# Score masks through two 64x128 array tiles in place of four 64x64 ones, and a new order of the same steps, in an attention and adapter kernel

## The chip, the core and the metric

The kernel runs on one core of a Trainium2 chip. The metric is the device time of one execution in microseconds. Three runs of the kernel before took 101.26, 102.77 and 100.77 us; the median is 101.26 us.

Five engines of the core work side by side, each through its own list of instructions: PE (matrix multiplication; its weight loads are shown as a row of their own, PEld), DVE (vector work), ACT (activation functions and copies), POOL (general work; here also the queue that issues the input loads) and SP (here only a DMA queue). They wait for one another by semaphores. PE writes into eight banks of accumulators (PSUM), 128 partitions by 512 fp32 values each.

## The reference

Eight batches, eight heads, 576 positions, head size 64. Attention looks back over a short window: heads 0 to 3 over the 32 positions up to the own one, heads 4 to 7 over every fourth of the last 128. The result goes through a mixture of eight low-rank adapters, of which each row takes its two best.

```python
rel = pos[:, None] - pos[None, :]
mask_plain = (rel >= 0) & (rel < window)                               # window 32
mask_dil = (rel >= 0) & (rel < window * dilation) & (rel % dilation == 0)  # dilation 4
scores = np.where(masks[None, :, :, :], scale * q @ k.T, -1e9)
attn = softmax(scores);  x = attn @ v          # then (B, S, H*D) -> rows of 512
logits = x @ w_gate;     w = softmax over the two largest logits
out = x + sum over the two chosen e of w[e] * ((x @ A[e]) @ B[e])      # rank 16
```

(`softmax` and the last line are shortened from longer code.)

## The kernel before

The host sorts the positions of the dilated heads by their remainder by four. A dilated window then looks like a plain one of 32 neighbours, cut at the borders of the four classes. So both kinds of head are a band: 64 keys against the 96 queries that can see them, nine such blocks per head, and a block's mask is a 64x96 pattern of 0 and -30000. `plain` holds the pattern twice, on partitions 0 to 63 and 64 to 127; `MD` holds nine copies for the dilated heads with the cuts put in. `CON` also holds a 128x128 identity, used to put masks into the banks and to transpose.

Work is cut by batch r (0 to 7) and head group g (0 plain, 1 dilated; four heads each). The two halves of the partitions hold two heads' keys and queries each. The steps have names, which the order and the prediction use:

- `gRGH`, `qRGH`, `vRGH`: loads of batch R, group G, half H, fp32 in memory and bf16 on chip, issued by POOL. At most eight are in flight. Three slots hold batches; batch r waits for the readers of batch r-3.
- `S0 r.g`, `S1 r.g`: scores of blocks 0 to 4 and 5 to 8, into a pair of banks, on PE. First come the masks (identity times pattern, starting the accumulation), then the score matmuls of 64x64 tiles, four tiles side by side (two heads by two partition halves).
- `E0`, `E1`: exponentials on ACT, from the pair of banks to the probabilities P (four buffers).
- `Va`, `Vb`: probabilities times values on PE, 128x128 tiles, the row sums in an extra column; `H`: the last 64 rows of a batch, in 128x64 tiles.
- `R`, `N` (`RH`, `NH`): reciprocal of the row sums and normalisation on DVE; `B`, `BH`: cast to bf16 on POOL.
- `T`, `TH` transposes on PE, `C`, `CH` their copies on ACT; `Z` the router and the adapters' A on PE, `ZC` its copies on ACT; `M`, `s12`, `tt`, `top`, `g2` the choice of the two best on DVE, `th` on ACT; `gz` the gated product on POOL; `GT`, `gc`, `gn` its transpose and copies; `D` the adapters' B on PE, `A` the addition on DVE.
- `st`: five stores on SP (batches 0 to 3, 4 and 5, 6, and 7 in two pieces), issued behind the last loads.
- Start-up: `con`, `bt` (SP) and `aw` (ACT) load constants and weights, `md` builds `MD` on DVE, `zero..`, `pz..`, `gz0.`, `xz.`, `fz` clear what must be zero.

The order of all steps is written out in the table `ORDER` (lines 52 to 89); `name@bank` says which bank a step takes. `replay` (line 154) walks the table and gives each engine its instructions in this order, so an engine never overtakes. While it does so it estimates times, only to decide where to put fillers: matmuls on zeros (`fz`) that stand in PE's list where PE is expected to be idle (`fill`, line 279). The cost terms in the code (`t`, `wired`) act on nothing else once the table is given.

All instructions are emitted through a helper, so the profile puts all of them on line 120; the tiles' names tell them apart (`con` or `md,con` into `ps`: masks; `kv` into `ps`: scores; `kv,p`: values; `aw,xt`: router and A; `bt,gn` and `bt,gc`: B; `fz`: filler).

Of the kernel before, what the change touches and what calls it, by code (L numbers as in the profile page):

```python
# [11 lines left out]
BF = mybir.dt.bfloat16  # L12
# [5 lines left out]
B, H, S, D = 8, 8, 576, 64  # L18
# [5 lines left out]
SEG = 96  # L24
PER = 192
CI = S // C
VW = D + 1
# [22 lines left out]
GZSPLIT = ()  # L50

ORDER = """
startACT aw land_aw startDVE zero01 zero11 pz00 pz30 pz11 pz20 gz00 pz21 zero00 startSP con land_con fz awc bt
land_bt xz0 md startPOOL g011 land_g011 g010 land_g010 S0_0.1@0 S1_0.1@2 pz10 q001 land_q001 E0_0.1 Va_0.2@0
q000 land_q000 v001 land_v001 E1_0.1 pz01 Vb_0.2 R_0.2 N_0.2 v000 land_v000 S0_0.0@2 g101 land_g101 S1_0.0@4
Va_0.3@6 g100 land_g100 Vb_0.3 E0_0.0 Va_0.0@2 g110 land_g110 g111 land_g111 E1_0.0 g200 land_g200 Va_0.1@0
g201 land_g201 Vb_0.0 zero10 R_0.0 g211 land_g211 table N_0.0 g210 land_g210 Vb_0.1 H_0@4 B_0.2 RH_0 NH_0 BH_0
TH_0@4 CH_0 btc R_0.1 N_0.1 S0_1.0@2 E0_1.0 S1_1.0@4 B_0.0 E1_1.0 R_0.3 N_0.3 B_0.1 T0_0@6 B_0.3 g301
land_g301 T1_0@7 C1_0 pz31 Va_1.1@2 g300 land_g300 Va_1.0@0 zero20 Vb_1.1 xz1 C0_0 Vb_1.0 S0_1.1@4 E0_1.1
R_1.1 N_1.1 Z0_0@6 ZC0_0 Z1_0@2 g311 land_g311 R_1.0 N_1.0 ZC1_0 B_1.1 M0_0 M1_0 top_0 s12_0 S1_1.1@4 E1_1.1  # L60
B_1.0 T0_1@6 g310 land_g310 tt_0 th_0 Va_1.2@2 g2_0 zero21 Va_1.3@0 Vb_1.2 R_1.2 gz0_0 N_1.2 Vb_1.3 R_1.3
N_1.3 S0_2.0@4 H_1@7 RH_1 B_1.2 NH_1 C0_1 S1_2.0@2 GT_0@6 B_1.3 gc_0 E0_2.0 E1_2.0 Va_2.0@4 Va_2.1@0 BH_1 g401
land_g401 Vb_2.0 gn_0 R_2.0 N_2.0 g400 land_g400 TH_1@2 CH_1 T1_1@3 C1_1 Vb_2.1 R_2.1 N_2.1 B_2.0 D0p_0@6
A0p_0 S0_2.1@4 E0_2.1 Z1_1@3 S1_2.1@0 E1_2.1 B_2.1 T0_2@2 C0_2 Va_2.3@6 Va_2.2@4 Vb_2.3 g410 land_g410 R_2.3
N_2.3 Vb_2.2 R_2.2 N_2.2 Z0_1@0 ZC1_1 M1_1 H_2@1 RH_2 ZC0_1 M0_1 g411 land_g411 NH_2 S0_3.0@6 B_2.3 s12_1 tt_1
D4_0@0 A4_0 g501 land_g501 S1_3.0@4 D2p_0@2 A2p_0 B_2.2 T1_2@1 E0_3.0 E1_3.0 Va_3.0@6 gz01 Va_3.1@4 BH_2 g500
land_g500 C1_2 th_1 Vb_3.0 top_1 g2_1 TH_2@0 CH_2 Vb_3.1 S0_3.1@2 R_3.1 R_3.0 N_3.0 N_3.1 E0_3.1 Z0_2@0 ZC0_2
M0_2 S1_3.1@6 E1_3.1 Z1_2@2 g511 land_g511 ZC1_2 gz0_1 GT_1@0 gc_1 gn_1 M1_2 s12_2 top_2 tt_2 th_2 Va_3.3@4
Va_3.2@6 Vb_3.3 R_3.3 Vb_3.2 B_3.1 B_3.0 T0_3@2 C0_3 R_3.2 N_3.3 S0_4.0@0 E0_4.0 N_3.2 g510 land_g510 H_3@3
RH_3 D2p_1@4 D4_1@2 S1_4.0@6 E1_4.0 g2_2 B_3.3 NH_3 g601 land_g601 A2p_1 A4_1 D0p_1@0 A0p_1 B_3.2 T1_3@3 C1_3  # L70
Va_4.1@4 Va_4.0@6 g600 land_g600 BH_3 TH_3@2 CH_3 Vb_4.1 Vb_4.0 R_4.1 R_4.0 N_4.0 S0_4.1@0 E0_4.1 gz0_2 GT_2@2
gc_2 gn_2 Z0_3@3 ZC0_3 N_4.1 M0_3 Z1_3@6 ZC1_3 M1_3 s12_3 Va_4.3@0 S1_4.1@4 g611 land_g611 E1_4.1 top_3 tt_3
th_3 D0p_2@2 A0p_2 S0_5.0@6 E0_5.0 B_4.1 B_4.0 g610 land_g610 g2_3 Va_4.2@4 Vb_4.3 gz0_3 Vb_4.2 R_4.3 N_4.3
S1_5.0@2 R_4.2 N_4.2 H_4@6 g700 land_g700 RH_4 NH_4 T0_4@7 E1_5.0 C0_4 Va_5.1@0 GT_3@2 gc_3 D4_2@3 A4_2 Vb_5.1
R_5.1 N_5.1 S0_5.1@4 D2p_2@6 B_4.3 g701 land_g701 B_4.2 T1_4@3 gn_3 D0p_3@0 E0_5.1 A2p_2 BH_4 TH_4@2 Va_5.0@4
g711 land_g711 C1_4 A0p_3 D2p_3@6 A2p_3 Vb_5.0 R_5.0 N_5.0 B_5.0 g710 land_g710 CH_4 Z1_4@2 ZC1_4 Z0_4@0 M1_4
ZC0_4 M0_4 s12_4 tt_4 S1_5.1@2 B_5.1 S0_6.0@6 Va_5.2@0 S1_6.0@4 top_4 E1_5.1 Vb_5.2 R_5.2 E0_6.0 th_4 g2_4
N_5.2 Va_5.3@2 Va_6.0@6 Vb_5.3 R_5.3 N_5.3 E1_6.0 Vb_6.0 R_6.0 N_6.0 H_5@4 RH_5 S0_6.1@0 S1_6.1@2 E0_6.1 gz0_4
GT_4@5 gc_4 E1_6.1 gn_4 Va_6.1@6 B_5.3 NH_5 B_5.2 Va_6.2@0 Vb_6.1 R_6.1 N_6.1 T0_5@2 C0_5 Vb_6.2 R_6.2 B_6.0
N_6.2 T1_5@5 C1_5 BH_5 TH_5@4 B_6.1 CH_5 D2p_4@6 B_6.2 S0_7.0@2 E0_7.0 A2p_4 Va_6.3@0 D4_3@5 Vb_6.3 A4_3 R_6.3  # L80
N_6.3 D0p_4@6 A0p_4 Z0_5@5 ZC0_5 Z1_5@2 ZC1_5 S1_7.0@0 E1_7.0 S0_7.1@4 Va_7.1@6 Va_7.0@2 Vb_7.1 B_6.3 T1_6@0
M0_5 M1_5 s12_5 tt_5 th_5 top_5 g2_5 gz0_5 Vb_7.0 R_7.1 N_7.1 B_7.1 R_7.0 N_7.0 B_7.0 E0_7.1 C1_6 S1_7.1@4
H_6@6 RH_6 GT_5@7 E1_7.1 Va_7.3@0 Va_7.2@2 Vb_7.3 T0_6@4 Vb_7.2 gc_5 gn_5 NH_6 BH_6 T0_7@5 TH_6@7 H_7@6 C0_6
R_7.3 N_7.3 B_7.3 CH_6 D0p_5@0 C0_7 R_7.2 N_7.2 Z0_6@7 RH_7 Z1_6@2 B_7.2 T1_7@3 D4_4@5 NH_7 A0p_5 ZC0_6 ZC1_6
D4_5@4 D2p_5@0 M0_6 BH_7 TH_7@2 M1_6 s12_6 tt_6 C1_7 th_6 top_6 CH_7 Z1_7@2 ZC1_7 A4_5 g2_6 gz0_6 Z0_7@4 A2p_5
ZC0_7 A4_4 GT_6@2 gc_6 gn_6 D4_6@2 M1_7 M0_7 s12_7 tt_7 th_7 top_7 g2_7 A4_6 D2p_6@4 A2p_6 st_0 land_st_0
D0p_6@0 A0p_6 st_4 land_st_4 gz0_7 GT_7@2 gc_7 gn_7 D0p_7@2 A0p_7 D2p_7@0 st_6 land_st_6 st_7a land_st_7a
A2p_7 D4_7@4 A4_7 st_7b land_st_7b
"""


def constants():
    k = np.arange(64)[:, None]
    w = np.arange(SEG)[None, :]
    m = np.where((w >= k) & (w - k < W), 0.0, NEG).astype(np.float32)
    m = np.concatenate([m, m], 0)
    return np.concatenate([m, np.eye(128, dtype=np.float32)], 1).astype(ml_dtypes.bfloat16)


class Op:  # L100
# [222 lines left out]
def attn_adapters_kernel(  # L323
# [12 lines left out]
    te, ve, se, ge, sy = (Noted(e, made) for e in (nc.tensor, nc.vector, nc.scalar, nc.gpsimd, nc.sync))  # L336
# [4 lines left out]
    def sb(shape, dt, name):  # L341
        return one.tile(shape, dt, name=name)
# [17 lines left out]
    TH = [sb([128, 5, 8], FP, f"th{i}") for i in range(2)]  # L360
    TOP = [sb([128, 5, 8], FP, f"top{i}") for i in range(2)]
    G2 = [sb([128, 5, 8], FP, f"g2{i}") for i in range(2)]
    CON = sb([128, SEG + 128], BF, "con")
    MD = sb([128, NB, SEG], BF, "md")
    FZ = sb([128, 512], BF, "fz")
    AWF = sb([128, 4 * (ER + E)], FP, "awf")
# [1 line left out]
    AW = sb([128, 4, ER + E], BF, "aw")  # L368
    BT = sb([128, H * D], BF, "bt")
    plain = CON[:, 0:SEG]  # L370
    ident = CON[:, SEG:]
    PS = [psum.tile([128, 2, 512], FP, name=f"ps{i}") for i in range(4)]

    def zero(view):
# [11 lines left out]
    add = plan.add  # L386

    def pe(cols, **kw):
        t = sum(max(c / 2400.0, 0.042) + 0.003 for c in cols)
        return dict(eng="PE", occ=t, lat=t + 0.25, **kw)  # L390
# [9 lines left out]

    wire = {"all": []}

    def wired(nbytes, pieces, issue, name, late=0.85):
        took = 0.97 * (nbytes / 438400.0 + 0.031 * pieces / 16 + 0.03)
        land = add("DMA", took, took + late, None, deps=[issue], prio=len(wire["all"]), name="land " + name)
        wire["all"].append(land)
        return land

    def early(eng, queue, dst, src, nbytes, name, deps=()):
        def emit():  # L410
            i = queue.dma_start(out=dst, in_=src)
            for d in deps:
# [7 lines left out]

    plan.first = {e: add(e, t, t, None, prio=-3000, name="start" + e)
                  for e, t in (("SP", 0.75), ("ACT", 0.72), ("POOL", 1.24), ("DVE", 0.9))}
    c_con = early("SP", sy, CON, con, 57000, "con")
    c_bt = early("SP", sy, BTF, bt, 262000, "bt")
    c_aw = early("ACT", se, AWF, aw, 278000, "aw")
    plan.first["ACT"] = add("ACT", 1.35, 1.35, None, prio=-1500, name="table")
    fz = add("DVE", 0.33, 0.45, lambda: ve.memset(zero(FZ), 0), prio=-70, name="fz")
# [54 lines left out]
    queued = []  # L482
# [3 lines left out]
    def load(r, half, c0, c1, deps, name):  # L486
        n = len(INST)
        INST[n] = None
        shift = 0 if half == 0 else QG + VN
        dst = T[r % SLOTS][(lo, hi)[half], c0:c1]  # L490
        src = rows[r, half, :, c0 - shift : c1 - shift]

        def emit():
            INST[n] = ge.dma_start(out=dst, in_=src)

        before = [queued[n - 8]] if n >= 8 else []
        issue = add("POOL", 0.55, 2.1, emit, deps=deps, prio=-1000 + n, name=name)
        issue.order_deps, issue.queued = before, True
        queued.append(wired(64 * (c1 - c0) * 4, 64, issue, name))
        return queued[-1]  # L500

    def vcols(half, g):
# [28 lines left out]
    pdone = {}  # L531
# [13 lines left out]
    def attention(r):  # L545
        for g in range(2):
# [8 lines left out]
            for part, (b0, nb) in enumerate(((0, 5), (5, 4))):  # L555
                k = Bank(2, 1)

                def scores(r=r, g=g, b0=b0, nb=nb, k=k):
                    o = pair(k)
                    for half in range(2):  # L560
                        hs = (lo, hi)[half]
                        for hh in range(2):
                            dst = o[(lo, hi)[hh], half, 0 : nb * SEG]
                            if g == 0:
                                m = plain[hs].unsqueeze(1).to_broadcast([64, nb, SEG])
                            else:
                                m = MD[hs, b0 : b0 + nb].rearrange("p b w -> p (b w)")
                            te.matmul(
                                dst, lhsT=ident[hs, 64 * half : 64 * half + 64], rhs=m,
                                start=True, stop=False, skip_group_check=True,  # L570
                            )
                    for j in range(nb):
                        b = b0 + j
                        n = SEG if b < NB - 1 else 64
# [5 lines left out]
                                    start=False, stop=(j == nb - 1), skip_group_check=True,  # L580
                                )

                t = nb * SEG / 2400 + 0.03 + nb * 0.056
                sc = add(
                    "PE", t, t + 0.25, scores, deps=klist + [c_con] + ([md] if g else []) + ([last] if last else []),
                    bank=k, prio=base + part, name=f"S{part} {r}.{g}", mode=1,
# [75 lines left out]
                        )  # L662

        base = 100.0 * r + 60
        hv = add(**pe([2 * VW] * 4), emit=halves, deps=pdone[2 * r] + pdone[2 * r + 1], bank=k, prio=base + 8, name=f"H {r}", mode=2)
        for g in range(2):
            pdone[2 * r + g].append(hv)
        att_done[r].append(hv)
# [297 lines left out]
```

## Time and profile before

| | |
|---|---|
| median of three runs | 101.26 us (100.77 to 102.77) |
| the profiled execution | 102.37 us, of which the span of the instructions is 100.6 us |
| PE busy | 83.6 us, 1577 matmuls |
| PE weight loads | 65.0 us, 1577 |
| DVE, ACT, POOL busy | 72.4, 63.5, 51.8 us |
| DMA | 24.50 MB, mean 244 GB/s |
| masks: `con` 64*64 64x480 and 64x384, `md,con` the same | 4 x 32 matmuls |
| scores: `kv` 64*64 | 576 matmuls |
| fillers: `fz` | 33 matmuls |

The profile is of one execution. It divides the span into 40 slices of 2.5 us and shows each engine's busy share in tenths. Matmuls overlap in the array and their ends are modelled, so their durations add up to more than the time they take; the distance from one start to the next says what a matmul costs. The chain of waits goes backwards from the last instruction to what released it; its shares say where time can be won or lost. A tile shape such as 64*64 means 64 rows by 64 columns of the array.

### The profile page before, as it was taken

Reading aid. Unit: us, or ns where it says so; the run is one execution under the profiler, and the core shown is the slowest. Engines: PE = TensorE matmul, PEld = TensorE weight load, DVE = VectorE, ACT = ScalarE, POOL = GpSimd, SP = SyncE. Lnnn points to the kernel's source line nnn. Section 1 sums busy time; section 2 is a strip of 40 time slices with the busy share of each in tenths; the row PEclk is TensorE's granted clock in tenths of the full one; section 3 lists DMA queues with packets and bytes.
Section 4 is the critical chain, followed back from the end, with each engine's and each line's share of the span. In section 5 each row is a group of like instructions: output and inputs, shape, how many; then the busy total and the mean of one; then the engine's idle time right before and its main releaser. Section 6 shows DMA issues by size and latency. Waiting matters only on the chain.

```text
span 100.6 us, 3747 instructions
## 1 busy us (share of the span) xinstructions
PE 83.6 (83%) x1577; PEld 65.0 (65%) x1577; DVE 72.4 (72%) x210; ACT 63.5 (63%) x109; POOL 51.8 (51%) x88
## 2 busy tenths in 40 slices
PE   0059799999999999998999999599799999887500
PEld 0021468487978978886987888387699897743300
DVE  5884012946596499877979999788698899787640
ACT  5600429299978969777797895629759998432000
POOL 5912254498797666747925940667423851531000
PEclk9999999999999999999999999999999999999965
DMA  2999999999999999999999999999459969299894
GB/s 51 311 196 189 218 215 213 208 216 219 216 213 211 210 219 213 218 211 213 211 219 219 210 210 219 210 216 214 84 238 454 425 285 469 80 410 469 352 415 171
DMA packets 3888, 24.50 MB, mean 244 GB/s; under 512 B 800, under 2 KB 800, under 8 KB 3488
## 3 DMA queue, kind: packets, MB, share of 16 engines
q0 software_dynamic: 2720, 14.23, 69.3%
q1 hardware_dynamic: 1008, 9.76, 23.3%
q8 instruction: 12, 0.20, 0.7%
q10 hardware_dynamic: 144, 0.28, 0.7%
q14 instruction: 4, 0.03, 0.1%
HBM read 29.06 MB, written 9.44 MB: 383 GB/s over the span
## 4 chain that ended last, share of the span: by engine, by line
PE 70%; DMA 9%; DVE 8%; issue 4%; ACT 2%; DVEq 2%; POOL 1%; ACTq 0%; POOLq 0%
PE ps L120 70%; DMA kv<-in_rows_dram 9%; DVE x L120 6%; DVEq L956 2%; ACT xt L120 1%; DVE gc L120 1%; POOL kv L120 1%; ACT gn L120 1%; DVE rec L120 0%; DVE mx L120 0%; DVE g L120 0%; ACT th L120 0%; DVE tt L120 0%; DVE s L120 0%; DVEq L120 0%
## 5 line engine op out<-in xcount | busy, mean ns | idle before, releaser
L120 ACT ACTIVATE p<-ps 128x960 bf16<-128x960 f32 (+1 forms) x32 | 27.8, 891 | 15.2 <-PE ps L120 12.4
L120 PE MATMUL ps<-kv,p 128*128 128x130 bf16 (+1 forms) x416 | 29.7, 223 | 0.8 <-issue 0.5
L120 POOL CAST xb<-x 128x512 bf16<-128x512 f32 x32 | 19.4, 614 | 15.9 <-DVE x L120 14.6
L120 PEld LDWEIGHTS <-p 128*128 128x128 bf16 (+1 forms) x416 | 23.9, 99 | 3.7 <-issue 1.4
L120 DVE TENSOR_TENSOR x<-x,ps 128x1024 f32<-128x1024 f32 (+1 forms) x24 | 21.9, 949 | 1.7 <-PE ps L120 1.6
L120 DVE TENSOR_TENSOR x<-ps,rec 128x512 f32<-128x512 f32 x32 | 21.9, 689 | 1.1 <-DVE rec L120 0.2
L120 POOL DMA_DIRECT2D kv<-in_rows_dram x34 | 17.9, 535 | 8.7 <-DMA kv<-in_rows_dram 6.9
L120 ACT COPY xt<-ps 128x128 bf16<-128x128 bf16 (+1 forms) x32 | 19.1, 647 | 3.8 <-DVE x L120 2.1
L120 DVE RECIPROCAL rec<-ps 128x8 f32<-128x8 f32 x32 | 6.4, 202 | 14.1 <-PE ps L120 13.7
L120 PE MATMUL ps<-fz 128*128 128x512 bf16 x33 | 10.8, 455 | 6.1 <-DVE fz L120 6.1
L120 POOL TENSOR_TENSOR gz<-zs,g 128x640 bf16<-128x640 f32 x8 | 10.2, 1275 | 11.0 <-DVE g L120 11.0
L120 PEld LDWEIGHTS <-kv 64*64 64x64 bf16 x576 | 11.1, 110 | 5.4 <-issue 2.0
L120 PE MATMUL ps<-kv 64*64 64x96 bf16 (+1 forms) x576 | 12.2, 206 | 2.5 <-issue 1.6
L120 PE MATMUL ps<-aw,xt 128*128 128x136 bf16 x160 | 11.2, 223 | 0.4 <-ACT xt L120 0.4
L120 PEld LDWEIGHTS <-xt 128*128 128x128 bf16 x160 | 9.7, 98 | 1.1 <-ACT xt L120 0.7
L120 PE MATMUL ps<-bt,gn 128*128 128x256 bf16 x40 | 9.6, 275 | 0.5 <-ACT gn L120 0.4
L120 PE MATMUL ps<-bt,gc 128*128 128x256 bf16 x40 | 9.6, 273 | 0.3 <-ACT gn L120 0.3
L120 PE MATMUL ps<-con,xb 128*128 128x128 bf16 x128 | 9.6, 219 | 0.0
L120 ACT COPY zs<-ps 128x408 f32<-128x408 f32 (+1 forms) x16 | 6.8, 446 | 4.2 <-PE ps L120 3.9
L120 PEld LDWEIGHTS <-fz 128*128 128x128 bf16 x33 | 3.2, 109 | 9.3 <-DVE fz L120 6.1
L120 ACT COPY gn<-ps 128x512 bf16<-128x512 bf16 (+1 forms) x16 | 5.6, 404 | 4.4 <-DVE gc L120 4.2
L120 PEld LDWEIGHTS <-xb 128*128 128x128 bf16 x128 | 7.6, 98 | 0.6 <-POOL xb L120 0.2
(36 smaller groups left out, 73.6 us busy)
## 6 DMA issues: line engine op xcount, KB each, us to landing
kv<-in_rows_dram POOLq DMA_DIRECT2D x30, 434.2 KB, 13.0
out_dram<-x SPq DMA_DIRECT2D x1, 4608.0 KB, 14.2
out_dram<-x SPq DMA_DIRECT2D x1, 2304.0 KB, 6.9
out_dram<-x SPq DMA_DIRECT2D x1, 1152.0 KB, 4.7
out_dram<-x SPq DMA_DIRECT2D x1, 640.0 KB, 2.9
kv<-in_rows_dram POOLq DMA_DIRECT2D x2, 288.0 KB, 10.1
out_dram<-x SPq DMA_DIRECT2D x1, 512.0 KB, 2.8
kv<-in_rows_dram POOLq DMA_DIRECT2D x2, 146.2 KB, 10.9
```

Source lines behind the costliest of these rows:

```text
L120: i = call(*args, **kw)
L956: with _tile.TileContext(nc) as tc:
```

## The change

Before, the masks of one score group were four matmuls, one for each 64x64 tile: for each half of the partitions (64 array rows, one bank) and each half of the output partitions. Now they are two, one for each half: the stationary operand `two` has two 64x64 identities side by side, so one matmul of a 64x128 tile writes the pattern to all 128 output partitions of a bank. The scores that follow are as before, in 64x64 tiles. The constants grow by 128 columns for `two`.

The table `ORDER` is replaced as a whole. It has the same steps, in other places and with other banks. Two terms of the estimate change with it.

```diff
-    return np.concatenate([m, np.eye(128, dtype=np.float32)], 1).astype(ml_dtypes.bfloat16)
+    two = np.tile(np.eye(64, dtype=np.float32), (2, 2))
+    return np.concatenate([m, np.eye(128, dtype=np.float32), two], 1).astype(ml_dtypes.bfloat16)
...
-    CON = sb([128, SEG + 128], BF, "con")
+    CON = sb([128, SEG + 256], BF, "con")
...
-    ident = CON[:, SEG:]
+    ident = CON[:, SEG : SEG + 128]
+    two = CON[:, SEG + 128 :]
...
-    def wired(nbytes, pieces, issue, name, late=0.85):
+    def wired(nbytes, pieces, issue, name, late):
...
-    c_con = early("SP", sy, CON, con, 57000, "con")
+    c_con = early("SP", sy, CON, con, 90000, "con")
...
-        queued.append(wired(64 * (c1 - c0) * 4, 64, issue, name))
+        queued.append(wired(64 * (c1 - c0) * 4, 64, issue, name, 0.25 + max(0.6, 1.4 - 0.025 * n)))
...
-                        for hh in range(2):
-                            dst = o[(lo, hi)[hh], half, 0 : nb * SEG]
-                            if g == 0:
-                                m = plain[hs].unsqueeze(1).to_broadcast([64, nb, SEG])
-                            else:
-                                m = MD[hs, b0 : b0 + nb].rearrange("p b w -> p (b w)")
-                            te.matmul(
-                                dst, lhsT=ident[hs, 64 * half : 64 * half + 64], rhs=m,
-                                start=True, stop=False, skip_group_check=True,
-                            )
+                        if g == 0:
+                            m = plain[hs].unsqueeze(1).to_broadcast([64, nb, SEG])
+                        else:
+                            m = MD[hs, b0 : b0 + nb].rearrange("p b w -> p (b w)")
+                        te.matmul(
+                            o[:, half, 0 : nb * SEG], lhsT=two[hs], rhs=m,
+                            start=True, stop=False, skip_group_check=True,
+                        )
...
-                t = nb * SEG / 2400 + 0.03 + nb * 0.056
+                t = nb * SEG / 2400 + 0.07 + nb * 0.056
```

The beginning of the two tables, up to the first values of the plain heads (of some 40 lines each):

```diff
-startACT aw land_aw startDVE zero01 zero11 pz00 pz30 pz11 pz20 gz00 pz21 zero00 startSP con land_con fz awc bt
-land_bt xz0 md startPOOL g011 land_g011 g010 land_g010 S0_0.1@0 S1_0.1@2 pz10 q001 land_q001 E0_0.1 Va_0.2@0
-q000 land_q000 v001 land_v001 E1_0.1 pz01 Vb_0.2 R_0.2 N_0.2 v000 land_v000 S0_0.0@2 g101 land_g101 S1_0.0@4
-Va_0.3@6 g100 land_g100 Vb_0.3 E0_0.0 Va_0.0@2 g110 land_g110 g111 land_g111 E1_0.0 g200 land_g200 Va_0.1@0
+startACT startSP con land_con md startDVE fz xz0 startPOOL aw land_aw zero00 pz11 awc pz00 g011 land_g011 pz01
+g010 land_g010 q000 land_q000 S0_0.1@0 v000 land_v000 q001 land_q001 S1_0.1@2 pz10 E0_0.1 zero01 Va_0.3@0
+Va_0.2@4 E1_0.1 Vb_0.2 pz21 pz31 R_0.2 N_0.2 v001 land_v001 S0_0.0@2 E0_0.0 S1_0.0@4 g100 land_g100 Va_0.1@2
+pz20 pz30 E1_0.0 Va_0.0@6 Vb_0.1 table Vb_0.0 xz1 R_0.0 N_0.0 zero10 g101 land_g101 g110 land_g110 Vb_0.3 g111
...
```

On the engines this gives: PE 1513 matmuls with their weight loads in place of 1577; 33 fillers as before, of which ten in place of seven stand ahead of the first score group; on DVE `md` is the first step in place of one behind nine clearing steps; on POOL the first batch's query and value loads come as q000, v000, q001, v001 in place of q001, q000, v001, v000; on ACT the two copies `zero10`, `zero11` stand together ahead of batch 1's exponentials in place of one at the start and one there; on SP the five stores keep their order, and the one for batches 4 and 5 stands ahead of the last batches' adapter steps in the table.

More of the change, by code (lines that the diff above doesn't have):

```diff
@@ L52 @@
 ORDER = """
-startACT aw land_aw startDVE zero01 zero11 pz00 pz30 pz11 pz20 gz00 pz21 zero00 startSP con land_con fz awc bt
-land_bt xz0 md startPOOL g011 land_g011 g010 land_g010 S0_0.1@0 S1_0.1@2 pz10 q001 land_q001 E0_0.1 Va_0.2@0
-q000 land_q000 v001 land_v001 E1_0.1 pz01 Vb_0.2 R_0.2 N_0.2 v000 land_v000 S0_0.0@2 g101 land_g101 S1_0.0@4
-Va_0.3@6 g100 land_g100 Vb_0.3 E0_0.0 Va_0.0@2 g110 land_g110 g111 land_g111 E1_0.0 g200 land_g200 Va_0.1@0
-g201 land_g201 Vb_0.0 zero10 R_0.0 g211 land_g211 table N_0.0 g210 land_g210 Vb_0.1 H_0@4 B_0.2 RH_0 NH_0 BH_0
@@ L58 @@
[L58 to L87, printed above, removed]
@@ L88 @@
-A2p_7 D4_7@4 A4_7 st_7b land_st_7b
+startACT startSP con land_con md startDVE fz xz0 startPOOL aw land_aw zero00 pz11 awc pz00 g011 land_g011 pz01
+g010 land_g010 q000 land_q000 S0_0.1@0 v000 land_v000 q001 land_q001 S1_0.1@2 pz10 E0_0.1 zero01 Va_0.3@0
+Va_0.2@4 E1_0.1 Vb_0.2 pz21 pz31 R_0.2 N_0.2 v001 land_v001 S0_0.0@2 E0_0.0 S1_0.0@4 g100 land_g100 Va_0.1@2
+pz20 pz30 E1_0.0 Va_0.0@6 Vb_0.1 table Vb_0.0 xz1 R_0.0 N_0.0 zero10 g101 land_g101 g110 land_g110 Vb_0.3 g111
+land_g111 g201 land_g201 zero11 B_0.2 H_0@4 g200 land_g200 zero20 g210 land_g210 g211 land_g211 R_0.3 N_0.3
@@ new lines @@
+B_0.3 RH_0 NH_0 S0_1.0@6 E0_1.0 S1_1.0@0 E1_1.0 B_0.0 BH_0 g300 land_g300 T1_0@4 C1_0 Va_1.0@6 R_0.1 N_0.1
+Va_1.1@2 TH_0@5 CH_0 Vb_1.1 B_0.1 R_1.1 N_1.1 B_1.1 Vb_1.0 R_1.0 N_1.0 T0_0@0 S0_1.1@4 S1_1.1@2 C0_0 E0_1.1
+E1_1.1 Z0_0@6 ZC0_0 Z1_0@4 Va_1.2@0 Va_1.3@2 ZC1_0 M1_0 M0_0 top_0 s12_0 Vb_1.3 R_1.3 Vb_1.2 R_1.2 N_1.2
+S0_2.0@4 E0_2.0 gz01 S1_2.0@6 tt_0 th_0 E1_2.0 N_1.3 H_1@0 RH_1 NH_1 zero21 g301 land_g301 B_1.0 Va_2.1@4
+T0_1@2 C0_1 g2_0 Va_2.0@0 B_1.2 B_1.3 T1_1@6 C1_1 BH_1 TH_1@7 CH_1 Vb_2.1 R_2.1 N_2.1 Vb_2.0 R_2.0 S0_2.1@2
@@ new lines @@
+gz00 N_2.0 E0_2.1 S1_2.1@4 E1_2.1 gz0_0 GT_0@7 gc_0 gn_0 Z1_1@6 bt land_bt ZC1_1 Va_2.3@2 g310 land_g310
+Va_2.2@0 Vb_2.3 R_2.3 N_2.3 g311 land_g311 btc B_2.3 Vb_2.2 R_2.2 N_2.2 H_2@6 S0_3.0@4 E0_3.0 RH_2 g401
+land_g401 g400 land_g400 D0p_0@2 NH_2 A0p_0 S1_3.0@0 B_2.2 E1_3.0 D2p_0@6 A2p_0 B_2.1 Z0_1@4 ZC0_1 M0_1 M1_1
+s12_1 tt_1 top_1 Va_3.0@0 T1_2@2 Vb_3.0 R_3.0 N_3.0 Va_3.1@6 B_2.0 T0_2@3 Vb_3.1 R_3.1 g411 land_g411 C1_2
+N_3.1 C0_2 BH_2 TH_2@2 CH_2 th_1 S0_3.1@4 E0_3.1 g2_1 S1_3.1@0 Z0_2@2 E1_3.1 ZC0_2 M0_2 Z1_2@4 ZC1_2 M1_2
@@ new lines @@
+top_2 s12_2 Va_3.2@6 Va_3.3@0 Vb_3.2 g410 land_g410 R_3.2 N_3.2 S0_4.0@4 E0_4.0 gz0_1 Vb_3.3 R_3.3 S1_4.0@2
+tt_2 th_2 N_3.3 g2_2 g500 land_g500 H_3@6 RH_3 Va_4.1@4 GT_1@7 gc_1 E1_4.0 NH_3 B_3.1 gn_1 Vb_4.1 R_4.1 N_4.1
+Va_4.0@2 B_3.0 g501 land_g501 T0_3@0 C0_3 Vb_4.0 R_4.0 N_4.0 B_3.2 B_3.3 T1_3@6 g510 land_g510 C1_3 D2p_1@4
+A2p_1 g511 land_g511 g611 land_g611 BH_3 TH_3@7 CH_3 D0p_1@0 A0p_1 S0_4.1@2 g600 land_g600 E0_4.1 Z0_3@7 ZC0_3
+M0_3 Z1_3@4 ZC1_3 Va_4.2@2 S1_4.1@0 E1_4.1 S0_5.0@4 E0_5.0 M1_3 top_3 s12_3 tt_3 D4_0@7 A4_0 gz0_2 GT_2@6 gc_2
@@ new lines @@
+Vb_4.2 th_3 R_4.2 N_4.2 gn_2 Va_4.3@0 B_4.1 g601 land_g601 g610 land_g610 B_4.0 T0_4@7 Vb_4.3 R_4.3 N_4.3
+S1_5.0@4 g2_3 E1_5.0 H_4@6 RH_4 NH_4 D0p_2@2 C0_4 S0_5.1@0 E0_5.1 A0p_2 D4_1@6 Va_5.1@4 A4_1 gz0_3 GT_3@7 gc_3
+gn_3 Vb_5.1 R_5.1 N_5.1 Va_5.0@2 S1_5.1@0 E1_5.1 BH_4 TH_4@6 CH_4 Vb_5.0 R_5.0 N_5.0 Va_5.2@4 B_4.3 B_4.2
+T1_4@7 Vb_5.2 R_5.2 g700 land_g700 Va_5.3@0 N_5.2 B_5.2 D2p_2@2 A2p_2 D4_2@6 C1_4 Z1_4@7 ZC1_4 M1_4 Vb_5.3
+R_5.3 Z0_4@4 D2p_3@2 A4_2 g710 land_g710 N_5.3 A2p_3 ZC0_4 S0_6.0@6 M0_4 g711 land_g711 s12_4 S0_6.1@0 E0_6.0
@@ new lines @@
+E0_6.1 tt_4 S1_6.0@4 E1_6.0 H_5@2 th_4 D0p_3@6 RH_5 NH_5 Va_6.0@0 B_5.3 g701 land_g701 A0p_3 T1_5@3 C1_5
+S1_6.1@4 Vb_6.0 E1_6.1 B_5.1 top_4 g2_4 R_6.0 N_6.0 B_5.0 T0_5@6 C0_5 Va_6.3@2 D4_3@7 BH_5 TH_5@4 CH_5 A4_3
+Vb_6.3 R_6.3 N_6.3 Va_6.2@0 gz0_4 GT_4@7 gc_4 gn_4 Vb_6.2 R_6.2 N_6.2 Va_6.1@4 B_6.3 Z1_5@6 B_6.2 ZC1_5 Vb_6.1
+R_6.1 N_6.1 Z0_5@2 ZC0_5 B_6.1 D2p_4@6 A2p_4 M0_5 M1_5 top_5 s12_5 tt_5 S0_7.0@0 E0_7.0 S0_7.1@2 E0_7.1 th_5
+H_6@4 RH_6 NH_6 B_6.0 S1_7.0@6 S1_7.1@0 D0p_4@2 E1_7.0 Va_7.1@4 E1_7.1 Va_7.0@6 Vb_7.1 BH_6 TH_6@0 T0_6@1 CH_6
@@ new lines @@
+Vb_7.0 g2_5 gz0_5 GT_5@0 C0_6 A0p_4 R_7.1 N_7.1 R_7.0 B_7.1 Va_7.2@2 gc_5 Va_7.3@4 Vb_7.2 N_7.0 B_7.0 R_7.2
+N_7.2 B_7.2 T1_6@1 Vb_7.3 R_7.3 N_7.3 gn_5 D0p_5@6 A0p_5 T0_7@0 H_7@2 RH_7 NH_7 B_7.3 C1_6 Z0_6@1 Z1_6@4 C0_7
+ZC0_6 T1_7@5 M0_6 ZC1_6 M1_6 D2p_5@0 s12_6 C1_7 tt_6 th_6 BH_7 D4_4@4 TH_7@2 CH_7 top_6 D4_5@6 Z1_7@5 ZC1_7
+Z0_7@7 ZC0_7 A4_4 st_0 land_st_0 g2_6 gz0_6 A2p_5 A4_5 st_4 land_st_4 GT_6@5 gc_6 gn_6 D4_6@5 M1_7 M0_7 s12_7
+tt_7 th_7 top_7 g2_7 A4_6 D0p_6@6 A0p_6 D2p_6@0 A2p_6 gz0_7 GT_7@5 gc_7 gn_7 D0p_7@4 st_6 land_st_6 A0p_7
@@ L89 @@
+st_7a land_st_7a D4_7@0 D2p_7@6 A2p_7 A4_7 st_7b land_st_7b
 """
@@ L664, in attention @@
         base = 100.0 * r + 60
-        hv = add(**pe([2 * VW] * 4), emit=halves, deps=pdone[2 * r] + pdone[2 * r + 1], bank=k, prio=base + 8, name=f"H {r}", mode=2)
+        hv = add(**pe([2 * VW] * 6), emit=halves, deps=pdone[2 * r] + pdone[2 * r + 1], bank=k, prio=base + 8, name=f"H {r}", mode=2)
         for g in range(2):
```

## The prediction, made before the changed kernel was run

> **What bounds the kernel now.** I read the 40 slices first, then the chain that ended last, then the waits, then PE's timeline.
>
> ```profile
> PE   0059799999999999998999999599799999887500
> DMA  2999999999999999999999999999459969299894
> ```
>
> A slice is 2.5 us. Loads keep the DMA engines full to about 70 us and stores fill most of the rest; PE is full from 7.5 to about 85 us. Two resources are full together, so the next view must say which leads.
>
> ```profile
> PE 70%; DMA 9%; DVE 8%; issue 4%; ACT 2%; DVEq 2%; POOL 1%; ACTq 0%; POOLq 0%
> ```
>
> The chain is PE 70%: it enters PE when the first rows land at 10.77 us, leaves it at 84.2 us but for a short step over DVE near 66, and then goes through the router and adapters of the last batch, DVE's adds and the last store. The loads still pace the beginning: two halves of 434.2 KB at about 215 GB/s (the slices' GB/s) make 4.14 us for one batch and head group, and the first score groups of successive loads start at 23.58 (S0 1.1), 27.74, 31.94, 36.43 and 40.38 us, steps of 3.9 to 4.5. PE stands idle or runs fillers before 23.58, then has no gap to 45 us; by S0 7.0 (72.22 us) it is behind the loads, which ended near 70. So PE's work after 23.58 us sets the end, almost one to one.
>
> ```profile
> PE ps L120 <- issue: 2.2, 3, 1.3
> ```
>
> In total, times and longest: 2.2 us in which PE stood for nothing that the profile shows (0.35 at 45.3, 1.25 at 63.6, 0.55 at 70.5 us).
>
> Now the score groups themselves: start, duration, tile shape, count. Starts are what to read, because durations overlap.
>
> ```profile
> 71.91 0.27 PE L120 MATMUL ps<-bt,gn 128*128 128x256 bf16 x1
> 72.02 0.27 PE L120 MATMUL ps<-bt,gc 128*128 128x256 bf16 x1
> 72.22 0.40 PE L120 MATMUL ps<-con 64*64 64x480 bf16 x4
> 72.45 0.38 PE L120 MATMUL ps<-kv 64*64 64x96 bf16 x20
> 72.76 0.46 PE L120 MATMUL ps<-kv,p 128*128 128x130 bf16 x5
> ...
> 75.40 0.36 PE L120 MATMUL ps<-con 64*64 64x384 bf16 x4
> 75.59 0.33 PE L120 MATMUL ps<-kv 64*64 64x96 bf16 x16
> 75.75 0.37 PE L120 MATMUL ps<-md,con 64*64 64x480 bf16 x4
> 75.95 0.38 PE L120 MATMUL ps<-kv 64*64 64x96 bf16 x20
> 76.27 1.09 PE L120 MATMUL ps<-kv,p 128*128 128x130 bf16 x16
> ...
> 78.27 0.33 PE L120 MATMUL ps<-kv 64*64 64x96 bf16 x16
> 78.53 0.43 PE L120 MATMUL ps<-kv,p 128*64 128x130 bf16 x8
> 78.89 0.45 PE L120 MATMUL ps<-con,gz 128*128 128x128 bf16 x5
> ```
>
> One 256-column matmul takes 0.11 (71.91 to 72.02), yet 0.20 pass before the mask at 72.22: 0.09 is the change of tile shape. Sixteen scores take 0.16 when another score group follows (75.59 to 75.75), 0.26 when the 128*64 tiles follow (78.27 to 78.53): 0.10 again. The eight matmuls at 78.53 run in pairs, 4 x 0.056, but last 0.36: 0.13 for a change in columns alone. Four masks of 480 columns need 0.20 inside the shape (75.75 to 75.95) and 0.23 just after a change (72.22 to 72.45): they run side by side, and the first group after a change pays 0.03 more.
>
> [...] 0.09 to 0.13 us per change, four tiles in the time of one. [...] the score weights begin to load at 72.25, 0.03 after the masks start. [...] The page's queue q8 has 12 packets and 0.20 MB[...]; that PE's 2.2 us are such fetches is not shown.
>
> **The change part by part.** (1) *Masks.* 32 score groups lose 2 matmuls and 2 weight loads each, 64 pairs of 1577. The columns streamed stay 480 or 384 per tile, so no array time goes if the two tiles overlap as the four do. Issue may fall: 20 scores in 0.21 us are about 0.01 a pair, 0.02 per group, at most 0.5 us over 26 groups.
>
> (2) *Shapes.* Masks now use 64-row, 128-column tiles, scores still 64x64. Every group has a change in its middle that it did not have, and a group that follows a group (75.59 to 75.75) changes back. Counted along both instruction orders, PE changes shape 61 times before and 93 times after. From S0 1.1 on, where PE leads, it is 52 against 75: 23 more. The trace has no change from 64x128 to 64x64. Below: nothing, if a change of columns alone with the same rows does not wait. Above: 0.13, the change of columns alone at 78.53. I take 0.10, the common value: 23 x 0.10 = 2.3 us. The scores of those 26 groups are now first after a change: 26 x 0.03 = 0.8 us. Less 0.5 for issue (1), it is +2.6 us; at 0.04 per change and no extra start it would be +0.4 to +0.9, at 0.13 it is 3.0 + 0.8 = +3.8.
>
> (3) *Groups before 23.58 us*: 6 groups, 9 more changes, 0.9 us. Their cover is the wait for loads (two fillers just before 23.58, six at 17.99 to 19.46, 1.5 us). If the cover were short, up to 0.9 us comes on top.
>
> (4) *Start.* The constants grow from 56.0 to 88 KB on SP's queue ahead of the load of the adapters' B[...]. On DVE the dilated mask, which waits for the constants (issued 0.75, landed 2.6 later, 3.4 us), now stands ahead of every memset, where DVE had 5 us of memsets before it. Queued behind it: filler zeros, value zeros, gaps of P: 0.54 + 1.2 + 0.27 + 0.17 + 2 x 1.03 + 4 x 0.44 = 6.0 us, ready near 10 with gaps. First user is ACT's exponential at 11.44 and PE's values at 12.76. Cost nothing; the cover is the first rows' landing at 10.77, with about 1 us to spare. Fillers remain 33, ten instead of seven ahead of the first scores, and they hide in the same wait. ACT's copies of zeros move into one 2.3 us pair before the exponentials of batch 1, whose rows land near 19.4; also nothing.
>
> (5) *Order.* Values, transposes and adapters take other places, and banks move. POOL's loads keep their sequence but for the first v's and q's; its queue of eight in flight is some 16 us deep (4 loads per 8.3 us), so a load behind a cast is not late. SP's five stores keep their order; the one of batches 4 and 5 moves ahead of the last adapters. The end keeps its chain: router of batch 7, gates, adapters, three adds, last store. I have no row that prices the order as a whole, so I take 0, with -0.7 to +0.7 (a third of the 2.2 us that PE stands idle either way).
>
> Sum: +2.6 us, rounded to 2.5 for overlap that I can't see. The profiled execution took 102.37 us (span 100.6 and 1.8 around it): 104.9 for one like it. It lies 1.1 above the median of three, 101.26, so the forecast is 101.26 + 2.5, about **103.7 us**.
>
> **The rivals.** *B, the inner change is free*: rows stay 64 and only the columns widen; the weights of the scores then load under the masks as at 72.25. Against: 78.53, where columns alone changed and 0.13 passed. It gives 101.26 less up to 0.5, 100.8 to 101.3. *C, faster*: the three stalls of PE (2.2 us) go, since there are 4% fewer PE instructions and the dense stretches lie elsewhere, and the inner change is free. Place: 45.3, 63.6, 70.5 us; price: 2.2 + 0.5. From 101.26 that gives 98.6. It decides only if the changes cost under 0.03 us each (2.7 less 23 x 0.03 is 2.0); against it speaks that the median run, shorter than the profiled one, may hold fewer stalls already. *D, the two masks run one after the other*: 0.20 or 0.16 more for 26 groups, 4.7 us on top of 2.5: 108.5. Against: the four tiles of before, with two row halves, overlap fully.
>
> **How the numbers follow.** A measurement of this kernel tells about 2%, 2.0 us, from no change; the runs before spread over 2.0 us. Main case 0.64, of which 0.54 end above +2% (103.3) and 0.10 below; B 0.18 (within 2%); C 0.10 (faster); D 0.08 (slower). So slower 0.62, same 0.28, faster 0.10. Main case alone: 102.0 to 105.8 (+3.8 and 0.7 for the order above). To leave out no more than 2 in 10, the range reaches down into B: 100.9 to 105.8; C and D are left out.
>
> **What would show it.** In PE's timeline after: masks as 64*128 x2; from mask start to first score 0.30 to 0.33 (480 columns) instead of 0.20 to 0.23; score groups back to back no longer 0.16 apart from the next mask but 0.26; score weights no longer loading 0.03 after the masks; PE still gapless from about 24 us and its last router matmuls near 88 instead of 85.8; first scores still near 10.8. B is right if mask to score stays at 0.23; D if it is 0.4. I am wrong in the sum if PE has new gaps after 24 us, or if the loads end much later than 70.

## The result, and the profile after

The changed kernel took 107.18 us (median of 4 runs, 106.45 to 107.86) against 101.88 us for the kernel before in the same session: ratio 1.061, 95% interval 1.048 to 1.074. Two later series on other chips gave 1.040 (1.034 to 1.046) and 1.050 (1.042 to 1.059). It is slower, as forecast, but by 4 to 6 us where 2.5 were forecast, and lies above the stated range of 100.9 to 105.8 us. All ratios here compare the faster executions of each kernel, those within 1.5% of its fastest; with all executions counted they move by up to 0.009, the first to 1.052. The profiled execution took 106.45 us, span 104.7: 4.1 us of span more than the one of before.

The page after, PE and DMA in 40 slices (now 2.6 us each):

```profile
PE   0079999999799999899959999899997797888000
DMA  2999999999999999999999999996999900599970
```

Loads and PE are full as before. New is the end of the DMA row: two empty slices (84 to 89 us) before the last stores, and a 7 and a 0 behind them. The score groups in PE's timeline of the changed kernel (start, duration, tile shape, count):

```profile
74.44 0.27 PE L121 MATMUL ps<-bt,gc 128*128 128x256 bf16 x1
74.65 0.38 PE L121 MATMUL ps<-con 64*128 64x480 bf16 x2
74.96 0.41 PE L121 MATMUL ps<-kv 64*64 64x96 bf16 x20
75.30 0.38 PE L121 MATMUL ps<-md,con 64*128 64x480 bf16 x2
75.60 0.41 PE L121 MATMUL ps<-kv 64*64 64x96 bf16 x20
75.94 0.43 PE L121 MATMUL ps<-kv,p 128*64 128x130 bf16 x8
```

Mask to score is 0.31 (74.65 to 74.96), where before it was 0.23 after a change and 0.20 without one. Twenty scores before the next mask take 0.34 (74.96 to 75.30); inside one shape they would be 20 x 0.0105 = 0.21. For masks of 384 columns the step from mask to score is 0.27, where before it was 0.19 after a change: 96 columns make the same 0.04 in both kernels. So the two 64x128 tiles run side by side, and the change from 64x128 to 64x64 costs about 0.1, as the main case had it. The weights show it too: those of the scores begin to load at 74.95, 0.30 after the masks, where before it was 0.03 after them.

Next, the last router matmuls of each kernel (PE's timeline), before and after:

```profile
85.77 1.36 PE L120 MATMUL ps<-aw,xt 128*128 128x136 bf16 x20 [0.42 <-ACT xt L120]
```

```profile
88.01 1.36 PE L121 MATMUL ps<-aw,xt 128*128 128x136 bf16 x20 [0.58 <-ACT xt L121]
```

PE arrives 2.24 us later. The other 1.86 us of the 4.1 come behind it: from these matmuls to the end of the span it is 14.8 us before and 16.7 after. The DMA issues of the two pages, with KB and the time from issue to landing, say where. Before:

```profile
out_dram<-x SPq DMA_DIRECT2D x1, 2304.0 KB, 6.9
out_dram<-x SPq DMA_DIRECT2D x1, 1152.0 KB, 4.7
out_dram<-x SPq DMA_DIRECT2D x1, 640.0 KB, 2.9
out_dram<-x SPq DMA_DIRECT2D x1, 512.0 KB, 2.8
```

After:

```profile
out_dram<-x SPq DMA_DIRECT2D x1, 2304.0 KB, 9.1
out_dram<-x SPq DMA_DIRECT2D x1, 1152.0 KB, 6.6
out_dram<-x SPq DMA_DIRECT2D x1, 640.0 KB, 4.7
out_dram<-x SPq DMA_DIRECT2D x1, 512.0 KB, 4.7
```

Each of the last four stores takes about 2 us longer from issue to landing, although the stores have the sizes and the order of before and SP issued the last one (640 KB) 2.30 us later, at 99.03 instead of 96.73, much as PE's delay of 2.24 has it.

### The profile page after: what moved, and what is told of

The parts are those of the page before. It is cut to its first block, busy times and chain, and to the rows that moved or that the text cites. A ratio compares the mean times of both kernels' runs of the same rounds, so it can differ in the third digit from the quotient of the medians.

```text
span 104.7 us, 3614 instructions
## 1 busy us (share of the span) xinstructions
PE 85.2 (81%) x1509; PEld 63.4 (61%) x1513; DVE 72.7 (69%) x210; ACT 62.6 (60%) x109; POOL 51.7 (49%) x88
## 4 chain that ended last, share of the span: by engine, by line
PE 53%; DMA 22%; DVE 9%; issue 5%; ACT 3%; DVEq 1%; POOL 1%; ACTq 0%
PE ps L121 53%; DMA kv<-in_rows_dram 19%; DVE x L121 5%; DMA con<-in_con_dram 3%; DVE md L121 1%; DVEq L956 1%; ACT xt L121 1%; ACT p L121 1%; DVE gc L121 1%; ACT gn L121 1%; POOL xb L121 1%; DVE rec L121 1%; POOL kv L121 0%; ACT th L121 0%; DVE mx L121 0%
## 5 line engine op out<-in xcount | busy, mean ns | idle before, releaser
L121 ACT ACTIVATE p<-ps 128x960 bf16<-128x960 f32 (+1 forms) x32 | 27.3, 891 | 15.6 <-PE ps L121 15.4
L121 ACT COPY xt<-ps 128x1024 bf16<-128x1024 bf16 (+1 forms) x32 | 18.9, 648 | 4.0 <-PE ps L121 3.6
L121 PE MATMUL ps<-fz 128*128 128x512 bf16 x29 | 9.9, 466 | 6.2 <-DVE fz L121 5.8
L121 PE MATMUL ps<-kv 64*64 64x96 bf16 (+1 forms) x576 | 12.1, 206 | 0.7 <-DMA kv<-in_rows_dram 0.7
L121 PEld LDWEIGHTS <-kv 64*64 64x64 bf16 x576 | 8.0, 106 | 7.1 <-issue 5.9
```

What stands on the lines that cost most here:

```text
L121: i = call(*args, **kw)
```

## The experiments

Ratios are to the kernel before, in the same series on the same chip; e1 to e13 number the runs. Below, "router to end" is the time from the last router matmuls to the end of the span.

### Masks alone, order alone, and the whole again

Masks alone (e1): the order and the fillers of before, the larger constants, and the two new masks. The main lines of the edit, shortened:

```diff
-                        for hh in range(2):
-                            dst = o[(lo, hi)[hh], half, 0 : nb * SEG]
...
+                        te.matmul(
+                            o[:, half, 0 : nb * SEG], lhsT=two[hs], rhs=m,
```

> The order of before with the masks of after: two 64x128 matmuls per score group, nothing else moved. Theory M (the change of tile shape inside a score group costs, and PE is the bound): in the trace of after, mask to first score is 0.30 and 0.27 us against 0.23 and 0.19 before, and scores to the next step 0.34 and 0.29 against 0.31 and 0.26, so about 0.11 us per group; 26 groups lie where PE leads, so +2.6 to +3.0 us against before. Theory O (most of the +5.3 comes from the new order): at most +1.5 us. Theory T (the end of the kernel, where the last stores wait for one another, doubles a delay of PE): +4 us or more.

Order alone (e2): the changed kernel with the four old masks.

> The order of after with the four 64x64 masks of before. Theory M: the order costs what is left of +5.3, about +2.3 to +2.7 us against before, part of it from ten cold fillers that hold up the first scores (they start with the data landed at 9.1 us and not before 10.6). Theory O: +4 us or more. Theory T: near 0 to +1, because the delay of PE that the end would double is gone.

The fillers called cold there start 0.43 us apart in the trace of after (6.18 to 6.61 us), and those behind the router 0.21 (89.63 to 89.84); the first scores start at 10.64.

And the changed kernel itself (e3):

> The changed kernel once more, for a second trace on this chip. If the 1.3 us by which two last packets of the final store came late in its first trace belong to the kernel, they are there again and the last store takes 4.7 us to land; if they belong to that execution, it takes about 3 us as in before. The ratio to before should be 1.05 to 1.07 either way.

Measured: masks alone 1.011 (1.005 to 1.017), order alone 1.011 (1.005 to 1.017), both 1.040 (1.034 to 1.046), below the 1.05 to 1.07 expected. None of the three theories holds: each part costs about 1.1 us and the whole some 4, so something belongs to neither part by itself. The trace of the masks-only kernel gives a first answer. Adding up the distances from each start to the next, gaps left out, masks and scores from S0 1.1 to the last router matmuls take 5.28 + 7.67 = 12.95 us before, and 7.46 + 8.07 = 15.53 with the new masks: 2.6 us more, the forecast number. All of PE's work in this stretch grows by less, from 59.6 to 61.6 us, since other steps get shorter (the transposes of the gated products, `con,gz`, by 0.4). PE also has gaps that this work can fill, and the end differs. In the second trace of the changed kernel the last store again takes 4.8 us to land and router to end is 16.7 us: the late landing belongs to the kernel.

The masks-only kernel has the long end too (16.6 us), the order-only kernel does not (14.9). What the first shares with the changed kernel is not the larger constants (all three have them) but the length of PE's list: 1513 pairs of weight load and matmul, against 1577. Queue q8, of the kind `instruction` on the page, has 12 packets of 16 KB in both kernels, of 0.88 to 1.21 us each, and 13 where PE's list alone is longer than before (1641 pairs, e8 below). So I take them for blocks of PE's instructions. Their times, from the traces:

| kernel | PE pairs | last q8 packet, us | last store issued, us | router to end, us | 640 KB landing, us |
|---|---|---|---|---|---|
| before | 1577 | 86.1 to 87.3 | 96.73 | 14.8 | 2.9 |
| after | 1513 | 96.5 to 97.4 | 99.03 | 16.7 | 4.7 |

Counted in matmuls that PE has started by then, the last packet comes at nearly the same place of both lists: about the 1519th and the 1508th. From the first packet to the last, 124 matmuls start to a packet in both. In a list of 1577 some 60 are still to come, and DMA is nearly idle (80 GB/s in the slice from 85.5 us); in a list of 1513 it is the very end, in the middle of the stores of batches 4 to 6 (390 and 413 GB/s in the slices from 94.2 and 96.8 us). In the other traces of these two lengths it lies between the 1502nd and the 1520th.

The packets also show how a block of 0.93 us puts the landing off by 1.8. A packet's DMA engine is not recorded, but the times fit together: after, a store packet of 18 KB ends at 96.48 us and took 1.20, its fifteen neighbours 0.69 to 0.72; the block runs from there to 97.40; the next store packet of 9 KB starts there and takes 0.73, the others 0.35. One of sixteen rows of packets so loses 0.50 + 0.93 + 0.38 = 1.8 us and stays behind. The last packets of the other rows end by 101.65 us, those of this row at 103.34. Why the two neighbours of the block are longer is not shown.

### The length of PE's list

Eight of the first fillers become nine short matmuls each: 64 pairs more, at about the same time for a filler. The edit, shortened, with two comments added:

```diff
+        filled.append(k)
+        if len(filled) > EARLY:          # EARLY = 8
             te.matmul(bank(k), lhsT=FZ[:, 0:128], rhs=FZ, ...)
+            return
+        for n in range(PIECES_OF):       # PIECES_OF = 9
+            w = 56
+            te.matmul(bank(k)[:, w * n : w * n + w], lhsT=FZ[:, 0:128], rhs=FZ[:, 0:w], ...)
```

In the changed kernel (e4):

> The changed kernel with 64 more PE matmuls: eight of the ten fillers ahead of the first scores become nine of 56 columns each, so PE's list is as long as that of before (1577 pairs) and the time of the fillers about the same. Theory F (a 16 KB instruction block is fetched over a DMA ring while the last store runs, because the list of 1513 pairs reaches its last block only at its very end, and the store's packets behind it land late): the fetch comes some 10 us earlier as in before, the last store lands in about 2.9 us instead of 4.7, and the time from the last router matmuls to the end is 14.8 us instead of 16.7: -1.5 to -1.9 us against the changed kernel, ratio to before 1.02 to 1.03. Rival G (the late packets come from the larger constants or from the stores' order): 4.7 us and ratio 1.04 stay.

In the masks-only kernel (e5):

> The order of before with the two 64x128 masks and 64 more short filler matmuls, so that the length of PE's list is that of before. Theory F: the end is 14.8 us after the last router matmuls, 1.8 less than in the masks-only kernel. PE's masks and scores still take 2.5 us more than before. Where PE stands for nothing shown (2.15 us in before, 0 in the masks-only kernel) is open: with 2 us of it the ratio is about 1.02, with none 0.99 to 1.00. Rival G: the end stays 16.7 us after the router and the ratio is 1.01 to 1.02.

In the kernel before, where nothing else is touched (e8):

> The kernel before with 64 more short filler matmuls ahead of the first values, nothing else. PE's list then has 1641 pairs, 128 pairs[...] more than the changed kernel, so its end lies at the same place in a block. Theory F: the last block is again fetched while the last store runs, the store lands in 4.5 to 4.7 us instead of 2.9, the end comes 16.5 to 16.7 us after the last router matmuls, and the kernel before becomes +1.5 to +1.9 us slower by fillers alone (ratio 1.015 to 1.02). Rival G: no change (ratio within 0.005 of 1), since neither masks, constants nor order are touched.

And, on the chip of the last one, the masks-only kernel without them (e9) and with them (e10), and the changed kernel (e11):

> The masks-only kernel (order of before, 1513 pairs) once more, on one chip with the next two. Theory F: it carries the late fetch, 16.5 to 16.7 us from router to end, and lies 1.5 to 1.9 us above the next kernel: ratio to before 1.02 to 1.03. If the first ratio (1.011) holds and the next one stays at 1.010, the late fetch costs nothing in the order of before.

> The masks-only kernel with 64 short fillers (1577 pairs) once more on this chip. Ratio to before 1.007 to 1.013 as in its first run; router to end 14.8 us. PE's masks and scores take 2.5 us more than in before; what does not show was time in which PE waited for loads.

> The changed kernel on this chip, for the sum: masks as shown (about +1.0 us, the masks-only kernel with 64 more), late fetch +1.8, and the order the rest. Ratio 1.04 to 1.06; router to end 16.5 to 16.7 us.

| kernel | PE pairs | ratio (95%) | router to end, us | 640 KB landing, us |
|---|---|---|---|---|
| before + 64 (e8) | 1641 | 1.020 (1.012 to 1.027) | 16.6 | 4.7 |
| masks only (e1) | 1513 | 1.011 (1.005 to 1.017) | 16.6 | 4.7 |
| masks only (e9) | 1513 | 1.018 (1.011 to 1.025) | 16.6 | 4.8 |
| masks only + 64 (e5) | 1577 | 1.010 (1.007 to 1.013) | 14.8 | 2.9 |
| masks only + 64 (e10) | 1577 | 0.999 (0.993 to 1.006) | 14.8 | 3.0 |
| order only (e2) | 1577 | 1.011 (1.005 to 1.017) | 14.9 | 3.0 |
| after (e11) | 1513 | 1.050 (1.042 to 1.059) | 16.6 | 4.6 |
| after + 64 (e4) | 1577 | 1.016 (1.010 to 1.021) | 14.9 | 3.0 |

In the last two columns theory F holds in every row and rival G falls; e3 and e7 (1513 pairs, 16.7 and 16.5 us) and e12 and e13 (1577, 14.9 us) agree. The ratios follow it less closely: e4 and e9 lie just below the 1.02 to 1.03 expected, and e10 came out at 0.999 where 1.007 to 1.013 were expected. The kernel before + 64 is the plainest: 64 filler matmuls alone bring 1 to 3% and the long end. In e8 the last block comes at the 1639th of 1641 matmuls, one block, 120 matmuls, later in a longer list. That a block is just 128 pairs is my estimate in the text above; the traces of before and after have 124 to a packet. The DMA part of e8's page shows one block more than the 12 of before, and the last store's landing:

```profile
q8 instruction: 13, 0.21, 0.8%
...
out_dram<-x SPq DMA_DIRECT2D x1, 640.0 KB, 4.7
```

The changed kernel with 64 more, the same line of its page:

```profile
out_dram<-x SPq DMA_DIRECT2D x1, 640.0 KB, 3.0
```

Two pairs at equal place of the last block give the masks' own price: without a late block 1.010 and 0.999 against 1, with one 1.018 against 1.020. That is between nothing and 1%, although PE has 2.0 us more to do. The last block, where it meets the stores, is worth 1.8 us in the traces, 1.8% in e9 against e10 and 2.0% in e8. But e1 against e5, on two chips, doesn't show it, so its price in time is less sure than the long end itself.

The 64 pairs take more off the changed kernel than the end explains: on the same chip as e4, the changed kernel with earlier loads (e7 below) had 1.044, that is 2.8 us above it. The same kernel as e7 with the 64 pairs (e12 below, another chip) had 1.015. PE's timeline of e11 shows the rest:

```profile
82.10 0.87 PE L121 MATMUL ps<-kv,p 128*128 128x130 bf16 x12 [1.48 <-issue]
```

PE stands for 1.48 us in the middle of a value step, waiting for nothing that the profile names. All four traces with this order and 1513 pairs stop at this same matmul: here, in the first one 1.28 us, in e3 and e7

```profile
81.49 0.87 PE L121 MATMUL ps<-kv,p 128*128 128x130 bf16 x12 [0.47 <-issue]
```

```profile
81.22 0.87 PE L125 MATMUL ps<-kv,p 128*128 128x130 bf16 x12 [1.48 <-issue]
```

The three traces with 64 more pairs have no such stop there. In all four a q8 packet ends 1.3 to 1.5 us before PE goes on (80.71 us in e11), as it does at each of the three stops of the kernel before (packets ending at 44.35, 63.45 and 69.50 us, PE going on at 45.67, 64.81 and 71.01). So these look like blocks that came late. Why this one is late so often is not shown, but the traces give a hint: the third block from the end starts 5.6 to 7.1 us after SP has issued the first store (4608 KB, 14 us to landing) in these four, and from 1.9 us before to 1.1 us after that issue in the eleven others. It seems to queue behind the store; no run moves the store to test it.

### The kernel before again

> The kernel before once more for a second trace. If the three stops of PE (0.35, 1.25, 0.55 us) belong to the places in its list, they are there again within 0.3 us of the same steps; if they belong to the execution, they are elsewhere or gone. The last store lands in 2.9 us and the end is 14.8 us after the last router matmuls.

In this second trace (e6) the span is 98.7 us and router to end 14.8. After 17 us PE has no stop without a cause in the profile. It waits for loads instead (PE's timeline):

```profile
31.96 0.24 PE L120 MATMUL ps<-kv 64*64 64x96 bf16 x4 [0.64 <-DMA kv<-in_rows_dram]
```

The three stops of the first trace belonged to that execution. The chain that ended last, with PE 70% and DMA 9% in the first trace, is here

```profile
DMA 43%; PE 25%; DVE 14%; issue 5%; POOL 4%; ACT 3%; DVEq 2%; ACTq 0%; POOLq 0%
```

Together with a wait of 0.67 for the exponentials and 0.63 for the last copy, PE has 1.9 us of gaps from S0 1.1 to the router here, and 0.9 in the masks-only kernel with 64 more (e5). From S0 1.1 to the router it takes 61.7 us here (22.18 to 83.87) and 62.3 in e5 (21.95 to 84.29): 1.7 us more work of all kinds, 0.65 us more time.

### The loads

The order of after issues loads later against POOL's other steps. The page gives their median time to landing, in the changed kernel:

```profile
kv<-in_rows_dram POOLq DMA_DIRECT2D x30, 434.2 KB, 9.3
```

It was 13.0 before, so fewer loads are in flight. The edit moves only the loads in the table (21 of 34 stand earlier among the other steps), and fixes the fillers to the places of after. A part of it:

```diff
-B_0.3 RH_0 NH_0 S0_1.0@6 E0_1.0 S1_1.0@0 E1_1.0 B_0.0 BH_0 g300 land_g300 T1_0@4 C1_0 Va_1.0@6 R_0.1 N_0.1
+B_0.3 RH_0 NH_0 S0_1.0@6 E0_1.0 S1_1.0@0 E1_1.0 B_0.0 BH_0 g300 land_g300 g301 land_g301 T1_0@4 C1_0 Va_1.0@6
...
+R_0.1 N_0.1 Va_1.1@2 TH_0@5 CH_0 Vb_1.1 B_0.1 g310 land_g310 R_1.1 N_1.1 B_1.1 Vb_1.0 R_1.0 N_1.0 T0_0@0
```

In the changed kernel (e7), then in the changed kernel with 64 more (e12), and beside it that kernel without the earlier loads (e13):

> The changed kernel with the input loads on POOL as early against the casts as in the order of before (for example the third batch's g310, g311 behind 6 and 8 steps of POOL instead of 13); all other steps, banks and fillers are those of after. Theory L (part of the order's cost is loads issued late, so that the queue runs shallow: landing in 9.3 us median against 13.0 before, loads ending 0.8 to 1.8 us later): landing near 12 to 13 us, no wait of PE for loads after 24 us, -0.7 to -1.7 us against the changed kernel, ratio to before about 1.025 to 1.035. If casts behind waiting loads hold PE instead, no gain: ratio 1.04 or more.

> The changed kernel with 64 more short fillers (no late fetch) and with POOL's loads as early against its other steps as in before. Theory L (the order's cost is loads issued late): landing 12 to 13.5 us, PE waits for loads after 24 us below 0.5 us against 1.7, and about 0.8 us less than the next kernel: ratio 1.00 to 1.01. Rival (the order costs by its other steps, or casts held behind loads take back what is won): ratio within 0.005 of the next kernel's.

> The changed kernel with 64 more short fillers once more, beside the kernel with earlier loads. Ratio to before 1.010 to 1.022 as in its first run; landing 9.3 to 10 us, 1 to 2 us of PE waiting for loads after 24 us, router to end 14.8 to 14.9 us.

Measured: e7 1.044 (1.038 to 1.050), landing 12.1 us: no gain, though the loads land as theory L had it and PE waits only 0.35 us for them. e12 1.015 (1.009 to 1.022), e13 1.020 (1.015 to 1.025) on one chip, landing 12.0 and 8.7 us. From S0 1.1 on, PE's waits for loads vanish in e12, and are 0.45 us in e13, less than the 1 to 2 us expected; the three traces of the changed kernel have 0.7 to 1.8. e12 lies above the 1.00 to 1.01 of theory L, and within 0.005 of e13 as the rival had it. That difference lies within the intervals: that the loads are part of the order's price is possible and not shown. The order's price itself, about 1% (e2; e4 and e13 against e5 and e10), is open. Changes of shape alone are not its cause: with the four old masks the new order has 49 of them, the old one 61. In e13 PE has 0.6 us more work between S0 1.1 and the router than in e5, mostly in scores (8.6 against 8.1), in e12 0.3.

## Why the prediction was right and wrong

*Shapes.* Right in the main. The forecast was 2.6 us more work for PE from S0 1.1 on. In the two profiled executions this work, gaps left out, is 59.6 and 61.8 us: 2.2 more. The masks alone, in the old order, bring 29 changes of shape where the forecast for the whole has 23, and 2.0 us (e1). The inner change was neither free (rival B) nor did the two masks run one after the other (rival D), and the weights of the scores stopped loading early, as forecast. The four masks before fill all four tiles, and the weights at 72.25 load 0.03 after their start; in the changed kernel it is 0.30. Why they load ahead in the one and not in the other is not shown.

*"So PE's work after 23.58 us sets the end, almost one to one."* Wrong. Of the 2.0 us more in e1, nothing to 1.0 shows in the time. The timeline of one execution had no gap to 45 us, and its three stops hid that PE and the loads were nearly level: in a second execution of before PE waited for loads and exponentials, and in e5, with the longer masks, such gaps are 1.1 us less. That "slower" was right is in good part luck: at most 1.0 of some 5 us comes from the cause it named.

*The step that failed: the end, and part (1).* The prediction said "The end keeps its chain" and counted 64 pairs fewer as a gain of at most 0.5 us. It had named the 12 packets of q8, and asked only whether PE's stops were such fetches. Fewer pairs moved the places of the blocks: the last is fetched amid the last stores (+1.8 us in the traces, shown by adding pairs to three kernels), and one is late near 80 us in all four traces of the new order with this length (0.5 to 1.5 us). Together they cost about 2.8 us (e7 against e4), more than the masks.

*Order: "I take 0, with -0.7 to +0.7".* It costs about 1.1 us, above that range, and no run shows why. "A load behind a cast is not late" was half wrong: loads did land sooner after a later issue, and PE waited 0.4 to 1.8 us for them from S0 1.1 on; that this sets the time is not shown.

*Rival C.* It put a gain on PE's stops going away with a shorter list. That the length of the list moves such stops was close; the sign was the other way.

*Start.* Held: first scores at 10.6 us against 10.8, with ten fillers and `md` first on DVE; the constants of 88 KB landed 2.8 us after their issue, those of 56 KB 2.6.

*A sum.* The lower end of the main case, 102.0, does not follow from its own terms: 101.26 + 0.4 - 0.7 is 101.0. The whole range reached below it anyway.

Sum from the runs: masks 0 to 1.0, order 1.1, blocks 2.8: 3.9 to 4.9 us, against 4.0 to 6.1% measured in three series. The 6.1 of the first series rests on few executions. None of the kernels tried is faster than the one before.

## What to carry to other kernels

When two resources are nearly level, a longer step costs only what the other one doesn't already impose (here 0.65 us for 1.7 us more work, e5 against e6): look for small waits in more than one execution before calling one engine the bound. A change in the number of instructions moves the places where blocks of them are fetched, as it did here (the last at 96.5 us in place of 86.1 with 64 pairs fewer); where DMA is full, check where the last blocks fall, and try a few idle instructions more or fewer before judging an order. When two halves of a change don't add up to the whole, look for what only their sum or both share, here the length of a list.

## What was not expected of the hardware

Sixty-four filler matmuls, issued while PE waits anyway, made a kernel 2% slower, or took 3% off another; the traces lead to the places of 16 KB instruction fetches of 0.9 to 1.2 us. One such packet of 0.93 us amid the stores put off their landing by 1.8 us, twice its own length: the store packets just ahead of it and just behind it took 0.9 us longer too. PE went on 1.3 to 1.5 us after the end of a late packet at each of the stops read above.
